# Row sums in three parts between additions, and a last copy shared by two engines

## The chip, the cores and the metric

The kernel runs on one core of a Trainium2 chip. A core has five engines with queues of their own: TensorE (matrix products, which end in PSUM), VectorE and ScalarE (element work; both read PSUM), GpSimd and SyncE (here they mostly issue transfers). Each engine works through its own queue in order and waits at an instruction until the counters named in it have been reached. The metric is the device time of one execution in microseconds.

## The reference

Two stages are joined. The first is a convolution along the sequence with weights that differ at each position: 8 batches of 4160 positions, 192 features in 8 heads, 7 taps. The weights of a position and head are a softmax over the 7 taps. The second stage takes each of the 33280 rows through two products to 1024 features, keeps the larger of the two, and multiplies by a third matrix.

```python
w = exp(weight_gen - max(weight_gen, axis=-1))
w = w / (sum(w, axis=-1) + 1e-09)                    # over the 7 taps
out = einsum('bshk,bskhg->bshg', w, windows(x_pad))  # 7 shifted copies of x
x = out.reshape(B * S, D)                            # 33280 x 192
out = maximum(x @ w1, x @ w2) @ w_out
```

## The kernel before

Each of the 128 partitions holds 260 consecutive rows, called columns. They are worked on in 17 batches: fifteen of 16 columns (0 to 14), one of 12 (15) and one of 8 (16). Work on a batch passes through all the engines.

- Weights: ScalarE takes the exponential of the batch (`exp_sum`, line 153). VectorE adds each run of 7 into `sum_t` (`red`, line 168, 8 sums per column). ScalarE takes the logarithm of the sums (`ln`, line 172). VectorE subtracts it from the raw weights (`shift`, line 177), and ScalarE takes the exponential again, which gives the normalised weights in bf16 (`weights`, line 191).
- Taps: VectorE multiplies the shifted copies of x by the weights (`mul`, line 211) and adds the 7 products in three additions (`adds`, lines 227, 233 and 236): 3 pairs, 2 pairs, and the last one, which writes `y_t`. The function `adds` takes a callback `beside(i, of)` and calls it ahead of each of the three additions, with i = 0, 1, 2 and of = 3. What the callback issues stands there in VectorE's queue.
- Transpose: a transposing transfer on SyncE's queue brings `y_t` into `yt`, features on the partitions. A small copy on GpSimd (`gate`, line 253) waits for it, and then GpSimd issues the next loads.
- Products: TensorE works through 260 tiles, three to a group (`hidden`). A tile is one chunk of 128 of the 1024 hidden features for the 8 columns of a unit (two chunks where a unit has 4 columns). With w2 - w1 in `wd`, max(h1, h2) is h1 + relu(x (w2 - w1)), so the kernel computes hidden tiles into the PSUM tiles hda, hdb and hdc (line 336), ScalarE takes their ReLU into `rd_t` (line 346), and the output is x (w1 w_out) plus the ReLU times w_out, summed in the PSUM tile op_ps (lines 388 and 376). ScalarE copies op_ps to `o_t` (`evac`, line 434), and SyncE stores it.

The order within a group g on TensorE is: hidden tiles a and b, the first output matmuls (`out_first`), hidden tile c, the second output matmuls (`out_second`). On ScalarE it is: ReLU a, ReLU b, a relay that waits for the first output matmuls and lets the second ones go, the softmax steps marked "before", ReLU c, the copy out of op_ps, the softmax steps marked "after". op_ps has a single buffer of two PSUM banks, as each of hda, hdb and hdc has, so the first output matmuls of a group wait until the copy of the group before has read it.

The softmax steps of ScalarE are placed by a table written out by hand, `SOFTMAX_AT`, with keys (group, 0 for before or 1 for after). The entry (16, 1), for example, holds l.5, the logarithm of batch 5. VectorE's order is written in `extra(t)`, called for each tile: the multiplications and additions of the next batch, with the subtractions of a later batch beside one half's additions and the sums of batch b + 3 beside the other half's. The first tiles of the program (16 of them) follow a list of their own, `OPENING`, of steps such as `lw.0.1` for a weight load.

A callback's part i of n is cut by `part` (line 157): columns n*i//of to n*(i+1)//of of the batch.

The results leave at the end by `rest_of_results`, and the very last pair of columns by a branch of `evac` of its own (lines 420 to 429): one copy on ScalarE of 2 x 192 columns out of two PSUM banks into `o_last`, and two stores, one on ScalarE's queue and one on SyncE's.

Of the kernel before, what the change touches and what calls it, by code (L numbers as in the profile page):

```python
# [9 lines left out]
FP32 = mybir.dt.float32  # L10
# [7 lines left out]
def _sub(base: bass.AP, off: int, dims):  # L18
    ap = [list(base.ap[0])] + [[int(s), int(c)] for s, c in dims]
    return dataclasses.replace(base, offset=base.offset + off, ap=ap)  # L20
# [3 lines left out]
def kernel(  # L24
# [9 lines left out]
    nc = tc.nc  # L34

    B, S, D = x.shape
    H, K = weight_gen.shape[2], weight_gen.shape[3]
    F = moe_w1.shape[1]
    P = 128
# [3 lines left out]
    HF = F // 2  # L43
# [8 lines left out]
    NB = len(BATCHES)  # L52

    def dcol(c):

        return (c + ROT) % CPP


    def pieces(b):
        n = BATCHES[b][1]  # L60
        at, done = [], 0
        for w in (4, 4, 4, 4) if b < 2 else (8, 8) if n == 16 else (8, 4) if n == 12 else (4, 4):
            at.append((done, w))
            done += w
        return at
# [14 lines left out]
    consts = ctx.enter_context(tc.tile_pool(name="consts", bufs=1))  # L80
# [76 lines left out]
    def part(b, i, of):  # L157

        n = BATCHES[b][1]
        c0, c1 = (4 * i, n if i else 4) if of == FIRST else (n * i // of, n * (i + 1) // of)  # L160
        h0, h1 = c0 * H, c1 * H
        return slice(h0, h1), h0 * K, [[K, h1 - h0], [1, K]]

    def red(b, i=0, of=1):
        if i == 0:
            s_ts[b] = psm.tile([P, BATCHES[b][1] * H], FP32, name="sum_t", tag="sum")
        hs, at, ap = part(b, i, of)
        nc.vector.reduce_sum(out=s_ts[b][:, hs], in_=_sub(e_ts[b], at, ap), axis=AX.X)  # L168
# [5 lines left out]
    def shift(b, i=0, of=1):  # L174
        hs, at, ap = part(b, i, of)
        w_t = _sub(wg_ts[b], at, ap)
        nc.vector.tensor_tensor(out=w_t, in0=w_t, in1=_sub(s_ts[b], hs.start, [[1, hs.stop - hs.start], [0, K]]),  # L177
                                op=ALU.subtract)
# [38 lines left out]
    def adds(b, o, first=False, beside=lambda i, of: None):  # L217


        w = dict(pieces(b))[o]  # L220
        n = w * D

        def taps(at, step, cnt):
            return _sub(m_t, K * o * D + at * n, [[step * n, cnt], [1, w * D]])

        beside(0, 3)
        nc.vector.tensor_tensor(out=taps(0, 1, 3), in0=taps(0, 1, 3), in1=taps(3, 1, 3), op=ALU.add)  # L227
        if first:
            return
        beside(1, 3)  # L230
        if b not in y_ts:
            y_ts[b] = py.tile([P, 16 * D], BF16, name="y_t", tag="y")
        nc.vector.tensor_tensor(out=taps(0, 2, 2), in0=taps(0, 2, 2), in1=taps(1, 5, 2), op=ALU.add)  # L233
        beside(2, 3)

        nc.vector.tensor_tensor(  # L236
            out=_sub(y_ts[b], o * D, [[64, 2], [P, 3 * w // 2], [1, 64]]),
            in0=taps(0, 1, 1), in1=taps(2, 1, 1), op=ALU.add,
        )
# [24 lines left out]
    def half(j):  # L264
        return slice(64 * j, 64 * j + 64)


    LEFT = (0, 1, 2, K - 1)

    def sum_transpose(u, i=None):  # L270

        b, o, n = UNITS[u]
        assert n == 4
        to = "h" if i == 0 else "o"
        yps = yps_of[u, i] = ps[to].tile([P, 1024], FP32, name="yps", tag="hd" if i == 0 else "op")
        ks = range(6) if i is None else range(3 * i, 3 * i + 3)
        for k in ks:
            for t in range(K):
                at = K * o * D + (t * 6 + k if i is None else (K * i + t) * 3 + k % 3) * P
                for r in range(2):  # L280
                    nc.tensor.matmul(  # L281
                        yps[:, r * 512 + k * 64:r * 512 + (k + 1) * 64],
                        lhsT=m_t[half(r), at:at + P], rhs=ident[half(r), half(r)],
                        start=(k == ks[0] and t == 0), stop=(t == K - 1),
                        skip_group_check=True,
                    )
# [62 lines left out]
    def column(c):  # L349

        for u, (b, o, n) in enumerate(UNITS):
            k = c - BATCHES[b][0] - o
            if 0 <= k < n:
                return u, k // 2, k % 2

    def place(p):

        u, i, _ = column(2 * p)
        b, o, n = UNITS[u]
        return BATCHES[b][0] + o + i, n // 2  # L360
# [55 lines left out]
    def evac(p, n):  # L416

        tile_, at = op_at[p]
        o = o_t[0]
        if p == NT // 2 - 1:  # L420

            nc.scalar.copy(out=_sub(o_last, 0, [[D, 2], [1, D]]),
                           in_=_sub(tile_, at, [[512, 2], [1, D]]))
            for j, eng in enumerate((nc.scalar, nc.sync)):
                eng.dma_start(
                    out=bass.AP(tensor=out.tensor, offset=dcol(place(p)[0] + 2 * j) * D, ap=[[CPP * D, P], [1, D]]),
                    in_=o_last[:, j * D:(j + 1) * D],
                )
            return
        runs = [[q for q in range(p, p + n) if column(2 * q)[0] == u]  # L430
                for u in range(column(2 * p)[0], column(2 * (p + n - 1))[0] + 1)]
        for qs in runs:
            c, h = place(qs[0])
            copied = nc.scalar.copy(out=_sub(o, c % 24 * D, [[D, len(qs)], [h * D, 2], [1, D]]),  # L434
                           in_=_sub(tile_, at + (qs[0] - p) * D, [[D, len(qs)], [512, 2], [1, D]]))
        stores = []
        for q in range(p, p + n):
            u, i, _ = column(2 * q)
            if u == NU - 2 and UNITS[u][2] == 8 and i % 2:
                stores.append((nc.sync, place(q)[0] - 1, [4 * D, 2], [1, 2 * D]))  # L440
            elif u < NU - 1 and i == UNITS[u][2] // 2 - 1:
                w = i + 1
                for k in range(0, 2 * w, w if u in PARTED else 2 * w):
                    stores.append((nc.sync, place(q)[0] - i + k, [1, (w if u in PARTED else 2 * w) * D]))
            if u == NU - 1:
                stores.append((nc.sync, place(q)[0], [2 * D, 2], [1, D]))
        for eng, c, *ap in stores:

            def issue(eng=eng, c=c, ap=ap, o=o):
                eng.dma_start(  # L450
                    out=bass.AP(tensor=out.tensor, offset=dcol(c) * D, ap=[[CPP * D, P], *ap]),
                    in_=_sub(o, c % 24 * D, ap),
                )

            if 3 <= u < NU - 3:
                held.append(issue)
            else:
                while u > 3 and held:
                    held.pop(0)()
                issue()  # L460
        return copied
# [81 lines left out]
    ident, swap = around[:, 0:P], around[:, 64:64 + P]  # L543
    zeros = consts.tile([P, PAD * D], BF16, name="zeros")
    gate = consts.tile([P, 1], FP32, name="gate")
    o_last = consts.tile([P, 2 * D], FP32, name="o_last")

    pstage = ctx.enter_context(ExitStack())
    stage = pstage.enter_context(tc.tile_pool(name="pstage", bufs=1))
# [2 lines left out]
    ws = {(kind, wi): stage.tile([P, w], FP32, name=f"ws{wi}{kind}") for kind, w in (("E", F), ("T", HF)) for wi in range(2)}  # L552
# [10 lines left out]
    def load_w(h, wi):  # L563

        wsrc = (moe_w1, moe_w2)[wi]
        return nc.sync.dma_start(
            out=ws["E", wi][:, h * HF:(h + 1) * HF],
            in_=bass.AP(tensor=wsrc.tensor, offset=h * HF, ap=[[F, P], [1, HF]]),
        )

    def load_last(h, wi):

        wsrc = (moe_w1, moe_w2)[wi]
        return nc.sync.dma_start(  # L574
            out=ws["T", wi][half(h), :],
            in_=bass.AP(tensor=wsrc.tensor, offset=P * F + h * HF, ap=[[F, 64], [1, HF]]),
        )
# [184 lines left out]
    def extra(t):  # L762

        u, k = TILES[t]
        b, o, n = UNITS[u]
        s = o + k

        if s == 0 and b + 1 < NB:
            mul(b + 1, 0)
        later = 0 if b < 4 else 5  # L770
        if s == later and b + 1 < NB:

            c = b + 1
            adds(c, 0, beside=lambda i, of: shift(c + 1, i, of) if c + 1 < NB else None)
        if s == 8 and b + 2 < NB:
            mul(b + 1, 8)
        if s == 8 + later and b + 2 < NB:
            adds(b + 1, 8, beside=lambda i, of: red(b + 3, i, 2) if b + 3 < NB and i < 2 else None)
        if s == 8 and b + 2 == NB:
            mul(b + 1, 4)  # L780
            adds(b + 1, 4)
        if k == n // 4 - 1 and 7 < u + 1 < NU:
            transpose(u + 1)

    def steps(g, tiles):

        for t in tiles:
            extra(t)
# [36 lines left out]
```

## Time and profile before

| | us |
|---|---|
| median of 3 runs | 405.34 (405.34 to 405.47) |
| the profiled execution's own time | 405.37 |
| its span | 403.6 |
| busy: TensorE | 394.8 (98%) |
| busy: VectorE | 369.1 (91%) |
| busy: ScalarE | 360.9 (89%) |

The profile is of one execution. The span runs from its first to its last recorded event; the time is a little longer. A row of a timeline gives start, length, engine, line, operation, tiles and shapes, and in brackets the idle time of the engine just before it with what ended it. A row of a group gives the count, then busy time, mean length in ns and idle time before. PE is TensorE, DVE VectorE, ACT ScalarE, POOL GpSimd; a q behind the name is an engine's queue of transfers. Lengths of VectorE and ScalarE rows overlap a little with the row behind, so costs are read from start to start; the ends of TensorE's rows are modelled.

### The profile page before, as it was taken

To read this page: it belongs to the slowest core of one execution; us is meant where nothing else is said; L and a number is where in the kernel's file an instruction comes from. 1 tells how busy PE (TensorE), PEld (TensorE's weight loads), DVE (VectorE), ACT (ScalarE), POOL (GpSimd) and SP (SyncE) were. 2 spreads that over 40 slices of the span, in tenths; PEclk is the share of its full clock that TensorE was granted. 3 is DMA by queue.
4 is the path that set the end of the run, shared out by engine and by line. 5 is a ranking of instruction groups with operands and counts; after the bars stand their busy time and mean duration, and the time that the engine had idled before them with its cause. 6 is when DMAs were issued, how large, how long until landed. Compare 5 with 4: busy or idle time off the path is not lost.

```text
span 403.6 us, 16321 instructions
## 1 busy us (share of the span) xinstructions
PE 394.8 (98%) x7499; PEld 321.3 (80%) x7499; DVE 369.1 (91%) x211; ACT 360.9 (89%) x466; POOL 72.3 (18%) x96
## 2 busy tenths in 40 slices
PE   7799999999999999999999999999999999999996
PEld 3589999777778777778777778877777877787996
DVE  5999999999999999999999999999999999998200
ACT  5999899999999989999899999989999899888872
POOL 3111031211122210222220122122012121200000
PEclk9999999999999999999999999999999999999999
DMA  8956468767768646864766667777457847558304
GB/s 262 222 140 151 120 124 167 183 164 133 190 110 222 182 79 129 240 187 80 217 187 107 141 192 193 99 215 198 81 115 228 178 80 200 141 106 193 104 31 169
DMA packets 60883, 63.16 MB, mean 157 GB/s; under 512 B 47641, under 2 KB 48665, under 8 KB 60816
## 3 DMA queue, kind: packets, MB, share of 16 engines
q1 hardware_dynamic: 52816, 40.15, 36.4%
q0 software_dynamic: 7856, 21.89, 27.4%
q8 instruction: 58, 0.95, 1.0%
q10 hardware_dynamic: 144, 0.10, 0.1%
q14 instruction: 9, 0.07, 0.1%
HBM read 36.55 MB, written 25.56 MB: 154 GB/s over the span
## 4 chain that ended last, share of the span: by engine, by line
PE 92%; ACT 5%; DMA 1%; SPq 1%; issue 0%
PE op_ps L376 42%; PE hdc L336 13%; PE hdb L336 13%; PE hda L336 13%; PE op_ps L388 8%; ACT rd_t L346 2%; DMA ws0E<-in_moe_w_dram 1%; PE hdp L336 1%; PE yps L281 1%; ACT en_t L191 1%; ACT yt L293 1%; ACT e_t L153 0%; ACT w1t L644 0%; SPq L574 0%; ACT w L622 0%
## 5 line engine op out<-in xcount | busy, mean ns | idle before, releaser
L376 PE MATMUL op_ps<-wo,rd_t 64*128 64x192 bf16 x4160 | 210.6, 243 | 0.0
L376 PEld LDWEIGHTS <-rd_t 64*128 64x128 bf16 x4160 | 181.0, 94 | 14.7
L211 DVE TENSOR_TENSOR m_t<-xb,en_t 128x10752 bf16<-128x10752 bf16 (+2 forms) x39 | 187.8, 4821 | 1.5 <-ACT en_t L191 1.4
L336 PEld LDWEIGHTS <-wd 64*128 64x128 bf16 x1824 | 96.8, 94 | 40.4 <-issue 2.5
L346 ACT ACTIVATE rd_t<-hdc 128x1024 bf16<-128x1024 f32 x82 | 84.1, 1025 | 17.8 <-PE hdc L336 16.2
L253 POOL CAST gate<-yt 128x1 f32<-128x1 bf16 x30 | 39.9, 1332 | 271.3 <-DMA yt<-y_t 271.3
L346 ACT ACTIVATE rd_t<-hda 128x1024 bf16<-128x1024 f32 x81 | 83.4, 1030 | 0.2 <-ACT o_t L434 0.2
L346 ACT ACTIVATE rd_t<-hdb 128x1024 bf16<-128x1024 f32 x81 | 83.5, 1031 | 0.0
L227 DVE TENSOR_TENSOR m_t<-m_t 128x4608 bf16<-128x4608 bf16 (+1 forms) x30 | 73.0, 2433 | 0.1
L336 PE MATMUL hdc<-yt,wd 64*128 64x512 bf16 (+1 forms) x552 | 67.9, 353 | 0.0
L434 ACT COPY o_t<-op_ps 128x384 f32<-128x384 f32 (+1 forms) x99 | 56.1, 577 | 12.4 <-PE op_ps L376 12.3
L336 PE MATMUL hdb<-yt,wd 64*128 64x512 bf16 (+1 forms) x540 | 67.1, 355 | 0.0
L336 PE MATMUL hda<-yt,wd 64*128 64x512 bf16 (+1 forms) x540 | 67.1, 355 | 0.0
L388 PE MATMUL op_ps<-w,yt 64*128 64x192 bf16 x780 | 55.5, 243 | 0.0
L388 PEld LDWEIGHTS <-yt 64*128 64x128 bf16 x780 | 39.0, 94 | 14.5 <-issue 0.3
L233 DVE TENSOR_TENSOR m_t<-m_t 128x3072 bf16<-128x3072 bf16 (+1 forms) x30 | 50.2, 1674 | 0.1
L191 ACT ACTIVATE en_t<-wg_t 128x896 bf16<-128x896 f32 (+3 forms) x48 | 35.7, 773 | 3.0 <-PE op_ps L376 2.0
L236 DVE TENSOR_TENSOR y_t<-m_t 128x1536 bf16<-128x1536 bf16 (+1 forms) x30 | 27.5, 916 | 0.6
L177 DVE TENSOR_TENSOR wg_t<-wg_t,sum_t 128x280 f32<-128x280 f32 (+6 forms) x46 | 22.2, 483 | 0.0
L168 DVE TENSOR_REDUCE sum_t<-e_t 128x64 f32<-128x448 f32 (+3 forms) x31 | 19.7, 639 | 2.3 <-ACT e_t L153 2.3
L125 POOL DMA_DIRECT2D xb<-in_x_dram x34 | 18.2, 537 | 17.3 <-ACT rd_t L346 11.0
L153 ACT ACTIVATE e_t<-wg_t 128x896 f32<-128x896 f32 (+2 forms) x18 | 15.9, 886 | 2.1 <-DMA wg_t<-in_weight_gen_dram 2.1
(40 smaller groups left out, 110.0 us busy)
## 6 DMA issues: line engine op xcount, KB each, us to landing
out_dram<-o_t SPq DMA_DIRECT2D x21, 768.0 KB, 4.3
xb<-in_x_dram POOLq DMA_DIRECT2D x30, 384.0 KB, 5.0
out_dram<-o_t SPq DMA_DIRECT2D x22, 384.0 KB, 3.7
wg_t<-in_weight_gen_dram POOLq DMA_DIRECT2D x13, 448.0 KB, 5.7
xb<-xb POOLq DMA_DIRECT2D x7, 288.0 KB, 5.1
wg_t<-in_weight_gen_dram SPq DMA_DIRECT2D x2, 448.0 KB, 5.2
xb<-in_x_dram POOLq DMA_DIRECT2D x4, 192.0 KB, 6.4
xs<-in_x_dram SPq DMA_DIRECT2D x1, 576.0 KB, 4.3
```

What stands on the lines that cost most here:

```text
L177: nc.vector.tensor_tensor(out=w_t, in0=w_t, in1=_sub(s_ts[b], hs.start, [[1, hs.stop - hs.start], [0, K]]), op=ALU.subtract)
L191: act = nc.scalar.activation(out=_sub(en_ts[b], (o * WGC + ((i or 0) * J + j) * N * K) * 2, [[2 * N, K], [2, N], [1, 2]]), in_=_sub(wg_ts[ ...
L211: return nc.vector.tensor_tensor(out=m_out, in0=x_in, in1=_sub(en_ts[b], at * H * 2, [[2, K * n * H], [0, G // 2], [1, 2]]), op=ALU.mult,)
L227: nc.vector.tensor_tensor(out=taps(0, 1, 3), in0=taps(0, 1, 3), in1=taps(3, 1, 3), op=ALU.add)
L233: nc.vector.tensor_tensor(out=taps(0, 2, 2), in0=taps(0, 2, 2), in1=taps(1, 5, 2), op=ALU.add)
L236: nc.vector.tensor_tensor(out=_sub(y_ts[b], o * D, [[64, 2], [P, 3 * w // 2], [1, 64]]), in0=taps(0, 1, 1), in1=taps(2, 1, 1), op=ALU.add,)
L253: nc.gpsimd.tensor_copy(out=gate, in_=yt[:, 0:1])
L336: nc.tensor.matmul(hid_out(t, f, j), lhsT=wd_at(j, s, f // 4, f % 4 * P, P), rhs=_sub(yt_ts[u][half(j), :], (s + j) % 3 * P, [[3 * P, w // ...
L346: relu_of[t0] = nc.scalar.activation(out=rd[:, k * 1024:(k + n) * 1024], in_=hd[:, at:at + n * 1024], func=AF.Relu)
L376: return nc.tensor.matmul(op_out(c), lhsT=rd[rows, k * 1024 + at:k * 1024 + at + P], rhs=wo[rows, f * D:(f + 1) * D], start=False, stop=(r ...
L388: nc.tensor.matmul(op_out(c + j), lhsT=yt_ts[u][half(j), (3 * i + (s + j) % 3) * P:(3 * i + (s + j) % 3 + 1) * P], rhs=w10[half(j), s * D: ...
L434: copied = nc.scalar.copy(out=_sub(o, c % 24 * D, [[D, len(qs)], [h * D, 2], [1, D]]), in_=_sub(tile_, at + (qs[0] - p) * D, [[D, len(qs)] ...
```

## The change

Sums: beside the additions of a batch's second half, `red` is now called in three parts, one ahead of each addition. Before it was called in two parts, ahead of the first and of the second addition. For 16 columns the parts were 8 and 8 columns (448 and 448 elements in) and are now 5, 5 and 6 (280, 280, 336).

Last copy: `o_last` becomes two tiles of 192 columns. ScalarE copies the first half and VectorE the second; ScalarE's queue stores the first, SyncE's the second.

Two more edits stand in the diff. `sum_transpose` sums four taps in place of seven where `adds` was called in its short form (`first`), for which a set `fewer` is kept; `load_w` and `load_last` learn a form for a whole row block and another queue. `OPENING` is not changed.

```diff
@@ adds
         if first:
+            fewer.add((b, o))
             return
@@
-    LEFT = (0, 1, 2, K - 1)
+    fewer = set()
@@ sum_transpose
+        taps = (0, 1, 2, K - 1) if (b, o) in fewer else range(K)
         for k in ks:
-            for t in range(K):
+            for t in taps:
@@ evac
-            nc.scalar.copy(out=_sub(o_last, 0, [[D, 2], [1, D]]),
-                           in_=_sub(tile_, at, [[512, 2], [1, D]]))
-            for j, eng in enumerate((nc.scalar, nc.sync)):
+            for j, (eng, copy) in enumerate(((nc.scalar, nc.scalar.copy), (nc.sync, nc.vector.tensor_copy))):
+                copy(out=o_last[j], in_=tile_[:, at + 512 * j:at + 512 * j + D])
                 eng.dma_start(
                     out=bass.AP(tensor=out.tensor, offset=dcol(place(p)[0] + 2 * j) * D, ap=[[CPP * D, P], [1, D]]),
-                    in_=o_last[:, j * D:(j + 1) * D],
+                    in_=o_last[j],
                 )
@@
-    o_last = consts.tile([P, 2 * D], FP32, name="o_last")
+    o_last = [consts.tile([P, D], FP32, name=f"o_last{j}") for j in range(2)]
@@ load_w
+        at, w = (0, F) if h == 2 else (h * HF, HF)
         return nc.sync.dma_start(
-            out=ws["E", wi][:, h * HF:(h + 1) * HF],
-            in_=bass.AP(tensor=wsrc.tensor, offset=h * HF, ap=[[F, P], [1, HF]]),
+            out=ws["E", wi][:, at:at + w],
+            in_=bass.AP(tensor=wsrc.tensor, offset=at, ap=[[F, P], [1, w]]),
         )
-    def load_last(h, wi):
+    def load_last(h, wi, act=0):
@@
-        return nc.sync.dma_start(
+        return (nc.scalar if act else nc.sync).dma_start(
@@ extra
         if s == 8 + later and b + 2 < NB:
-            adds(b + 1, 8, beside=lambda i, of: red(b + 3, i, 2) if b + 3 < NB and i < 2 else None)
+            adds(b + 1, 8, beside=lambda i, of: red(b + 3, i, 3) if b + 3 < NB else None)
```

## The prediction

> **What bounds the kernel now.** I read the page's busy shares first, then its groups, then the waits of TensorE and ScalarE after the opening, and last the timelines of the places that the change touches.
>
> ```profile
> span 403.6 us, 16321 instructions
> PE 394.8 (98%) x7499; PEld 321.3 (80%) x7499; DVE 369.1 (91%) x211; ACT 360.9 (89%) x466; POOL 72.3 (18%) x96
> L376 PE MATMUL op_ps<-wo,rd_t 64*128 64x192 bf16 x4160 | 210.6, 243 | 0.0
> ```
>
> TensorE is busy 98% of the span, and its largest group has no idle time ahead of it. From 60 us on, the list of what TensorE waited for is empty. So the end is set by TensorE's work plus the last copy and store. VectorE and ScalarE cost nothing unless one makes TensorE wait. VectorE is the engine to suspect: from about 39 us it runs without a gap to the end of its long work. The rows below say how far ahead of TensorE it still is late in the span.
>
> ```profile
> 349.83 1.75 POOL L253 CAST gate<-yt 128x1 f32<-128x1 bf16 x1 [9.17 <-DMA yt<-y_t]
> 351.83 0.83 PE L336 MATMUL hda<-yt,wd 64*128 64x512 bf16 x6
> ```
>
> GpSimd's gate starts when the transposed tile of batch 14's second half has landed; TensorE's first matmuls on that tile start 2.0 us later. VectorE's products arrive in time even there, by 2 us, so a faster VectorE shortens nothing, and up to 2 us more on it would be covered.
>
> **What the edits come to.** The set `fewer` stays empty, because no step of the opening asks for the short form of the additions; the new forms of the weight loads are not called either. These edits issue the same instructions as before, so they cost nothing and remove nothing. What is left is the sums and the last copy.
>
> **The sums on VectorE.** For batches 4 to 16 (13 of them) two reductions become three: 13 more instructions. In a batch of 16 columns, two of 448 elements become 280, 280 and 336. The rows below are one batch half with sums as it is now, and then the neighbouring half with three subtractions in the same places.
>
> ```profile
> 80.20 0.61 DVE L168 TENSOR_REDUCE sum_t<-e_t 128x64 f32<-128x448 f32 x1
> 80.73 2.55 DVE L227 TENSOR_TENSOR m_t<-m_t 128x4608 bf16<-128x4608 bf16 x1
> 83.20 0.62 DVE L168 TENSOR_REDUCE sum_t<-e_t 128x64 f32<-128x448 f32 x1
> 83.72 1.75 DVE L233 TENSOR_TENSOR m_t<-m_t 128x3072 bf16<-128x3072 bf16 x1
> 85.51 0.96 DVE L236 TENSOR_TENSOR y_t<-m_t 128x1536 bf16<-128x1536 bf16 x1
> ...
> 92.06 0.44 DVE L177 TENSOR_TENSOR wg_t<-wg_t,sum_t 128x280 f32<-128x280 f32 x1
> 92.42 2.56 DVE L227 TENSOR_TENSOR m_t<-m_t 128x4608 bf16<-128x4608 bf16 x1
> ...
> 95.24 1.75 DVE L233 TENSOR_TENSOR m_t<-m_t 128x3072 bf16<-128x3072 bf16 x1
> 96.91 0.50 DVE L177 TENSOR_TENSOR wg_t<-wg_t,sum_t 128x336 f32<-128x336 f32 x1
> 97.33 0.95 DVE L236 TENSOR_TENSOR y_t<-m_t 128x1536 bf16<-128x1536 bf16 x1
> ```
>
> From start to start the present half takes 0.53 + 2.47 + 0.52 + 1.79 = 5.31 us up to its third addition. The half with three subtractions takes 0.36 + 2.46 + 0.36 + 1.67 + 0.42 = 5.27. The third addition needs the second one's result: directly behind it, it starts 1.79 us after it; with a subtraction between, that subtraction starts after 1.67. A reduction of 336 lasts 0.50 us (the row at 316.87, below), the same as the subtraction of 336, so I price the new half as the subtracting half: 0.04 us less per batch, 0.5 us less on VectorE over 13 batches. Bounds: 1.6 us less over all, if only the 0.12 us of the waiting addition counts; 1.8 us more, if it isn't saved and each third reduction pays the part of a reduction that doesn't shrink with its size (0.61 for 448 and 0.50 for 336 leave about 0.14). All of it lies beside TensorE's work, under the 2.0 us above: nothing on the path.
>
> [...]
>
> **The logarithm that waits.** The sums feed one logarithm per batch on ScalarE (L172), placed by hand. Until now the last sum stood ahead of the second addition, now behind it. For batch 5 the third reduction starts at 80.20 - 0.04 (saved on batch 4) + 0.36 + 2.47 + 0.36 + 1.67 = 85.02 and ends at 85.52; today's second one ends at 83.20 + 0.62 = 83.82.
>
> ```profile
> 84.64 0.31 ACT L172 ACTIVATE sum_t<-sum_t 128x128 f32<-128x128 f32 x1
> 84.85 1.02 ACT L346 ACTIVATE rd_t<-hda 128x1024 bf16<-128x1024 f32 x1
> 85.75 1.03 ACT L346 ACTIVATE rd_t<-hdb 128x1024 bf16<-128x1024 f32 x1
> 86.75 1.02 ACT L346 ACTIVATE rd_t<-hdc 128x1024 bf16<-128x1024 f32 x1
> 87.67 0.47 ACT L434 COPY o_t<-op_ps 128x384 f32<-128x384 f32 x1
> ...
> 88.48 0.43 PE L388 MATMUL op_ps<-w,yt 64*128 64x192 bf16 x6
> ```
>
> ```profile
> 4.72 1.15 DVE L168 TENSOR_REDUCE sum_t<-e_t 128x64 f32<-128x448 f32 x2 [2.28 <-ACT e_t L153]
> 5.38 0.26 ACT L172 ACTIVATE sum_t<-sum_t 128x64 f32<-128x64 f32 x1 [0.22 <-DVE sum_t L168]
> ```
>
> ```profile
> 79.34 0.51 ACT L434 COPY o_t<-op_ps 128x384 f32<-128x384 f32 x1
> ...
> 79.90 0.42 PE L388 MATMUL op_ps<-w,yt 64*128 64x192 bf16 x6
> ```
>
> In the opening a logarithm starts about 0.05 us behind its reduction (4.72 + 0.61, then 5.38). So this one starts at 85.57 instead of 84.64: ScalarE stands still for 0.93 us. Queued behind it are the three ReLUs of the next group and the copy out of op_ps. At their present spacing (0.21, 0.90, then 0.91 and 0.92 without a wait) they start at 85.78, 86.68, 87.59 and 88.51; the copy ends at 88.98 where it ended at 88.14. The first output matmul of the group after that needs op_ps back. That it can start 0.05 us after such a copy is shown at 79.34 + 0.51 = 79.85 and 79.90. So it starts at 89.03 instead of 88.48: TensorE loses 0.55 us. The relay ahead of the second output matmuls (queued behind the ReLU at 86.68) may stop TensorE sooner, but that pause is part of the same 0.55, since the copy's end doesn't move with it. Lower bound: 0, if ScalarE's queue catches up; upper bound: the whole 0.93. I take 0.55, for op_ps has a single buffer and the rows have no other slack. TensorE has no later idle time to give it back.
>
> The other logarithms:
>
> ```profile
> 198.53 0.61 DVE L168 TENSOR_REDUCE sum_t<-e_t 128x64 f32<-128x448 f32 x1
> 203.25 0.31 ACT L172 ACTIVATE sum_t<-sum_t 128x128 f32<-128x128 f32 x1
> ```
>
> ```profile
> 245.87 0.61 DVE L168 TENSOR_REDUCE sum_t<-e_t 128x64 f32<-128x448 f32 x1
> 252.35 0.34 ACT L172 ACTIVATE sum_t<-sum_t 128x128 f32<-128x128 f32 x1
> ```
>
> ```profile
> 316.87 0.50 DVE L168 TENSOR_REDUCE sum_t<-e_t 128x48 f32<-128x336 f32 x1
> 320.90 0.28 ACT L172 ACTIVATE sum_t<-sum_t 128x96 f32<-128x96 f32 x1 [0.55 <-PE op_ps L376]
> 321.46 1.03 ACT L346 ACTIVATE rd_t<-hdc 128x1024 bf16<-128x1024 f32 x1 [0.28 <-PE hdc L336]
> ```
>
> Batch 10: the first reduction at 198.53 - 0.24, the last end 5.36 us later, 203.65. The logarithm would wait 0.45 us at its old time; but ScalarE and TensorE come 0.55 later, VectorE does not, so at 203.80 it finds its sums. Batch 12 (251.0 against 252.35) has more than 1 us, and so have the rest. Batch 15 (three reductions of 224 elements, about 5.1 us) ends near 321.55 against 320.90 + 0.55: up to 0.15 us, which the 0.28 us wait of the next ReLU covers. Nothing more is added.
>
> **The last copy.** The built program gives VectorE's copy one wait, on ScalarE's counter at the value that ScalarE's own half sets: both read the same op_ps tile. The halves follow each other; they do not run at once.
>
> ```profile
> 399.95 0.39 SPq L450 DMA_DIRECT2D out_dram<-o_t  x1
> 400.05 0.48 ACT L422 COPY o_last<-op_ps 128x384 f32<-128x384 f32 x1
> 400.56 0.34 SPq L425 DMA_DIRECT2D out_dram<-o_last  x1
> 400.56 0.37 ACTq L425 DMA_DIRECT2D out_dram<-o_last  x1
> ```
>
> ```profile
> 400.90:401.50 0.60, 0.00 (x0) 1.00 0.97 319
> 401.50:402.10 0.60, 0.00 (x0) 1.00 0.94 314
> ```
>
> ```profile
> L667 ACT CAST w<-pw 64x192 bf16<-64x192 f32 x2 | 0.6, 314 | 0.0
> L177 DVE TENSOR_TENSOR wg_t<-wg_t,sum_t 128x224 f32<-128x224 f32 x3 | 1.2, 385 | 0.0
> ```
>
> ScalarE's 192 columns take 0.31 us instead of 0.48, so its store is issued at 400.40, 0.16 earlier. VectorE has no copy out of PSUM in this trace; between 0.31 (ScalarE, same size) and 0.39 (a subtraction of 224) I take 0.35: from 400.41 to 400.76, and SyncE's store at 400.79, 0.23 later than now. What does that do to the end? The stage table (length, ScalarE's busy time, clock, DMA share, GB/s) shows the 16 DMA engines full from 400.9 to 402.1 with the store issued at 399.95 and these two. Issue to full flow is about 0.9 us (399.95 to 400.9), so SyncE's 96 KB flow from about 401.7, and at 319 GB/s need 0.3 us: 402.0, inside the present 402.1. I take 0; bounds 0.16 less and 0.23 more. Nothing is queued behind the two waiting stores but the end of the program.
>
> **Sum.** 0.55 + 0 + 0: the span goes from 403.6 to 404.15 us. The profiled execution took 405.37, 1.8 more than its span and 0.03 above the median of 405.34. On the median that is 405.9 us, 0.14% slower. A change below 0.2% (0.8 us) is about what a measurement of this kernel can't tell from none.
>
> **The rivals.**
> - The whole stall reaches TensorE. Its place is op_ps behind the logarithm of batch 5, its price 0.93 us, and with the late store of SyncE 1.16: 406.3 to 406.5, slower. It decides once the 0.34 us between the copy's end (88.14) and the matmul (88.48) hide less than 0.1. For it: the single buffer. Against: the pair at 79.85 and 79.90, which shows that 0.05 is enough.
> - The stall is absorbed: ScalarE runs early or the reductions end sooner; then 405.2 to 405.4. Against: ReLU rows at 84.85 to 87.67 without gaps.
> - The stall as forecast, and SyncE's store is late by its 0.23: 406.1. For it: the series. Against: full DMA engines.
> - The halves run at once: 0.55 - 0.16 gives 405.7. The Trainium skill, PSUM — Partial Sum Buffer (PSUM bank collisions raise a hardware error), has reads of different banks by two engines run clean; the halves lie in two banks. The wait in the program stands against it, and no row here shows it.
> - VectorE's tiles do hold TensorE: 0.5 us less, and no stall seen: 404.8. Against: the 2.0 us.
>
> **Chances.** Forecast 0.52, full stall 0.14, absorbed 0.14, late store 0.13, halves at once 0.03, VectorE the bound 0.04. The first, third, fourth and fifth lie within 0.2%, less a few hundredths at the edge of 406.15: same 0.78, slower 0.17, faster 0.05. The range 405.2 to 406.5 reaches from the absorbed to the full stall.
>
> **What would show it.** In the changed profile: a logarithm of batch 5 near 85.6 with a wait on L168 of 0.8 to 0.9 us; the output matmuls after it near 89.0; from there every TensorE row 0.5 to 0.6 later; 44 reductions; third additions 0.42 behind a reduction; VectorE's last copy behind ScalarE's. I am wrong if TensorE's rows past 90 us keep their times, if several logarithms wait, or if the last store ends more than 0.2 us later after the last matmul.

## The result and the profile after

The changed kernel takes 408.58 us (median of 8 executions, 407.28 to 410.62) against 405.4 us before: ratio 1.0078, 95% interval 1.0053 to 1.0102. It is slower by 0.8%; the forecast was 405.9 us, at most 406.5. The profiled execution took 409.53 us with a span of 407.8, so it holds 4.2 us more of span than the profiled execution of before.

These are the span, the busy shares and two groups on the page of the changed kernel:

```profile
span 407.8 us, 16334 instructions
PE 396.8 (97%) x7499; PEld 320.5 (79%) x7499; DVE 369.3 (91%) x225; ACT 360.2 (88%) x466; POOL 184.2 (45%) x96
...
L254 POOL CAST gate<-yt 128x1 f32<-128x1 bf16 x30 | 151.8, 5060 | 163.7 <-DMA yt<-y_t 163.7
...
L211 DVE TENSOR_TENSOR m_t<-xb,en_t 128x10752 bf16<-128x10752 bf16 (+2 forms) x39 | 187.8, 4821 | 12.2 <-ACT rd_t L348 9.2
```

The same gate group stood on the page of before like this:

```profile
L253 POOL CAST gate<-yt 128x1 f32<-128x1 bf16 x30 | 39.9, 1332 | 271.3 <-DMA yt<-y_t 271.3
```

VectorE and ScalarE are as busy as before (369.3 against 369.1 us, 360.2 against 360.9). The number that moved is GpSimd's: 184.2 us instead of 72.3, all of it in the gate, a copy of one column whose mean length went from 1.33 to 5.06 us. And VectorE's multiplications (L211) have 12.2 us of idle time ahead of them.

The waits of the changed kernel from 60 us to the end show what follows from that (engine, line, what it waited for; total us, times, longest us):

```profile
DVE m_t L211 <- ACT rd_t L348: 9.2, 1, 9.2
...
ACT sum_t L172 <- DVE sum_t L168: 4.7, 3, 2.2
DVE m_t L211 <- DMA xb<-xb: 2.8, 2, 1.7
...
PE op_ps L390 <- ACT o_t L435: 1.3, 3, 0.5
```

Three logarithms wait for their sums (4.7 us), where the forecast had one; VectorE waits for loads of x, which nobody had forecast. (The 9.2 us stands at 375.76, near the end of VectorE's work. The list puts it down to ScalarE's ReLU, but nearly all of it belongs to a long gate; the rows are further down.)

Matching TensorE's 7499 rows of both traces one by one shows where the changed kernel falls behind, as steps in the difference of starts:

| place (time in the trace of before) | TensorE later by | what it waits for |
|---|---|---|
| opening, up to 17 us | 1.2 us | loads of the weights |
| 88.5 | 0.49 | logarithm of batch 5 |
| 205 to 207 | 1.4 | logarithm of batch 10 |
| 323.9 | 0.7 | logarithm of batch 15 |
| 380 to 386 | 0.43 | the transposed tile yt |

The sum is 4.2 us. The first line belongs to this execution and not to the change: the opening's code issues the same instructions, and in the other profiles below the opening stands between 0.2 us early and 0.5 us late. Without it 3.0 us are left, which agrees with the medians (408.58 - 405.4 = 3.2).

Batch 5 in the changed kernel, as the forecast had it (all 1.2 us later than there because of the opening):

```profile
86.19 0.50 DVE L168 TENSOR_REDUCE sum_t<-e_t 128x48 f32<-128x336 f32 x1
86.60 0.95 DVE L237 TENSOR_TENSOR y_t<-m_t 128x1536 bf16<-128x1536 bf16 x1
86.72 0.31 ACT L172 ACTIVATE sum_t<-sum_t 128x128 f32<-128x128 f32 x1 [0.77 <-DVE sum_t L168]
...
89.65 0.49 ACT L435 COPY o_t<-op_ps 128x384 f32<-128x384 f32 x1
90.19 0.42 PE L390 MATMUL op_ps<-w,yt 64*128 64x192 bf16 x6 [0.31 <-ACT o_t L435]
```

And batch 10, which was to find its sums (a later window of the same timeline):

```profile
136.71 5.76 DVE L211 TENSOR_TENSOR m_t<-xb,en_t 128x10752 bf16<-128x10752 bf16 x1 [1.72 <-DMA xb<-xb]
...
206.24 0.50 DVE L168 TENSOR_REDUCE sum_t<-e_t 128x48 f32<-128x336 f32 x1
206.78 0.31 ACT L172 ACTIVATE sum_t<-sum_t 128x128 f32<-128x128 f32 x1 [1.72 <-DVE sum_t L168]
...
210.24 0.42 PE L390 MATMUL op_ps<-w,yt 64*128 64x192 bf16 x6 [0.46 <-ACT o_t L435]
```

VectorE has lost time at 136.71, where a multiplication starts 1.72 us late because its x is not there; by batch 10 its sums come too late and TensorE pays. Why x is late is seen where a load is issued. The clearest place is an earlier one. These rows are VectorE's and GpSimd's in the changed kernel from the third addition of batch 4's second half on:

```profile
62.59 0.50 DVE L168 TENSOR_REDUCE sum_t<-e_t 128x48 f32<-128x336 f32 x1
63.00 0.95 DVE L237 TENSOR_TENSOR y_t<-m_t 128x1536 bf16<-128x1536 bf16 x1
63.86 5.75 DVE L211 TENSOR_TENSOR m_t<-xb,en_t 128x10752 bf16<-128x10752 bf16 x1
69.28 12.19 POOL L254 CAST gate<-yt 128x1 f32<-128x1 bf16 x1 [9.85 <-DMA yt<-y_t]
69.53 0.45 DVE L177 TENSOR_TENSOR wg_t<-wg_t,sum_t 128x280 f32<-128x280 f32 x1
...
75.68 5.75 DVE L211 TENSOR_TENSOR m_t<-xb,en_t 128x10752 bf16<-128x10752 bf16 x1
81.35 0.44 DVE L168 TENSOR_REDUCE sum_t<-e_t 128x40 f32<-128x280 f32 x1
81.42 0.53 POOL L125 DMA_DIRECT2D xb<-in_x_dram  x1
```

And here is the same place in the kernel before:

```profile
60.06 1.75 DVE L233 TENSOR_TENSOR m_t<-m_t 128x3072 bf16<-128x3072 bf16 x1
61.85 0.96 DVE L236 TENSOR_TENSOR y_t<-m_t 128x1536 bf16<-128x1536 bf16 x1
62.72 5.75 DVE L211 TENSOR_TENSOR m_t<-xb,en_t 128x10752 bf16<-128x10752 bf16 x1
68.02 0.49 POOL L253 CAST gate<-yt 128x1 f32<-128x1 bf16 x1 [9.81 <-DMA yt<-y_t]
68.39 0.44 DVE L177 TENSOR_TENSOR wg_t<-wg_t,sum_t 128x280 f32<-128x280 f32 x1
68.56 0.53 POOL L125 DMA_DIRECT2D xb<-in_x_dram  x1
```

In both kernels the gate's transfer lands late in a long multiplication (5.75 us). Before, the copy ends 0.12 us after the next VectorE instruction has started (68.02 + 0.49 = 68.51 against 68.39). After the change, it does not get in there. It passes six further instructions of VectorE and a second long multiplication, and ends 0.12 us after a reduction has started (69.28 + 12.19 = 81.47 against 81.35). The load of x queued behind it on GpSimd (L125) is issued at 81.42 instead of 68.56. This first late load costs VectorE only 0.15 us at its next multiplication (87.69). The wait of 1.72 us at 136.71 comes about in the same way: a gate starts at 115.54 and lasts 13.37 us, and the loads behind it are issued from 128.85 on.

The 9.2 us near the end are such a wait too:

```profile
353.41 10.25 POOL L254 CAST gate<-yt 128x1 f32<-128x1 bf16 x1 [6.50 <-DMA yt<-y_t]
```

Behind this gate GpSimd issues loads at 363.60 and 364.12, and when the second has landed, at 371.23, the last transfer into x (L145), which lands 4.4 us later, at about 375.6; the multiplication starts at 375.76. In the run below that has the new sums and the old copy, the gate at this place got in early (352.35, 2.67 us), and the same multiplication waited 0.80 us. So over 8 of the 9.2 us belong to the gate. TensorE's last step (380 to 386) is what reaches TensorE of this wait.

The Trainium skill, SBUF — State Buffer (SBUF: two separate sides), states that VectorE and GpSimd have one port pair in common, that a VectorE instruction with two operands in SBUF competes for it with a GpSimd instruction that reads SBUF, that whichever starts first holds it for the whole instruction, and that the other is fully blocked. Multiplications, additions and subtractions here have two such operands, a reduction has one; that the copy gets through at a reduction, 0.12 us after its start, agrees. What the Trainium skill does not say there, and the trace shows, is that the hold can outlast the instruction: here eight VectorE instructions, one directly behind the other, keep the copy out, for 12 us. So the question of the experiments was which part of the change does this, and through what.

### The profile page after: what moved, and what is told of

Read it like the earlier page. It is cut to its first block, busy times and chain, and to the rows that moved or that the text cites. A ratio compares the mean times of both kernels' runs of the same rounds, so it can differ in the third digit from the quotient of the medians.

```text
span 407.8 us, 16334 instructions
## 1 busy us (share of the span) xinstructions
PE 396.8 (97%) x7499; PEld 320.5 (79%) x7499; DVE 369.3 (91%) x225; ACT 360.2 (88%) x466; POOL 184.2 (45%) x96
## 4 chain that ended last, share of the span: by engine, by line
DVE 61%; DMA 11%; PE 11%; issue 10%; ACT 5%; SPq 0%; POOL 0%; DVEq 0%; POOLq 0%; ACTq 0%
DVE m_t L211 28%; DVE m_t L227 14%; DVE m_t L234 10%; PE op_ps L378 5%; DVE y_t L237 5%; DMA yt<-y_t 4%; DMA xb<-xb 3%; ACT rd_t L348 3%; DVE wg_t L177 2%; DVE sum_t L168 2%; DMA wg_t<-in_weight_gen_dram 2%; DMA ws0T<-in_moe_w_dram 2%; PE hdc L338 1%; PE op_ps L390 1%; DMA xb<-zeros 1%
## 5 line engine op out<-in xcount | busy, mean ns | idle before, releaser
L254 POOL CAST gate<-yt 128x1 f32<-128x1 bf16 x30 | 151.8, 5060 | 163.7 <-DMA yt<-y_t 163.7
L211 DVE TENSOR_TENSOR m_t<-xb,en_t 128x10752 bf16<-128x10752 bf16 (+2 forms) x39 | 187.8, 4821 | 12.2 <-ACT rd_t L348 9.2
L125 POOL DMA_DIRECT2D xb<-in_x_dram x34 | 18.2, 537 | 18.8 <-ACT rd_t L348 10.9
L168 DVE TENSOR_REDUCE sum_t<-e_t 128x40 f32<-128x280 f32 (+6 forms) x44 | 21.7, 494 | 2.2 <-ACT e_t L153 2.2
```

The lines of the kernel that those rows point to most:

```text
L211: return nc.vector.tensor_tensor(out=m_out, in0=x_in, in1=_sub(en_ts[b], at * H * 2, [[2, K * n * H], [0, G // 2], [1, 2]]), op=ALU.mult,)
L254: nc.gpsimd.tensor_copy(out=gate, in_=yt[:, 0:1])
```

## The experiments

The theory was formed in this order: first which of the two edits loses the time, then whether the gate is the carrier, then what in VectorE's queue shuts the gate out. Each median stands beside that of executions of the kernel before, taken together with it on the same chip.

**One edit at a time.** The first run has the changed kernel's last copy and the old sums, the second the reverse.

```diff
e1: adds(b + 1, 8, beside=lambda i, of: red(b + 3, i, 2) if b + 3 < NB and i < 2 else None)
e2: adds(b + 1, 8, beside=lambda i, of: red(b + 3, i, 3) if b + 3 < NB else None)
e2: o_last = consts.tile([P, 2 * D], FP32)      # one copy on ScalarE, as before
...
```

> Sums in two parts as before, last copy shared as in the change. Both theories, starved gate and late logarithms, put nothing here: 405.2 to 405.7, the last row of SyncE's store about 0.4 us later behind the last matmul than before, no gate on GpSimd longer than 2 us. If the copy were part of the loss, 406 or more.

> Sums in three parts, last copy as before. Both theories: the whole loss, 407 to 410, with gates of 10 to 14 us in the trace and three logarithms that wait for VectorE. If the copy had a part in it, less than that.

The copy alone: 405.46 against 405.48 us, ratio 1.0006 (0.9995 to 1.0017). The sums alone: 408.82 against 405.48, ratio 1.0093 (1.0070 to 1.0116). The sums carry the whole loss, the copy none, though it runs as a series just as forecast. The end of the changed kernel:

```profile
404.29 0.32 ACT L425 COPY o_last<-op_ps 128x192 f32<-128x192 f32 x1
404.64 0.36 DVE L425 COPY o_last<-op_ps 128x192 f32<-128x192 f32 x1 [17.09 <-ACT o_last L425]
405.02 0.34 SPq L426 DMA_DIRECT2D out_dram<-o_last  x1
```

VectorE's half starts when ScalarE's has ended, and SyncE's store is issued 0.73 us behind the first half's start, 0.22 us later than before (400.05 to 400.56), where about 0.4 was expected. In the run with the copy alone TensorE's rows past 20 us stand within 0.1 us of before, and the span is 403.4 us against 403.6: the end does not move.

**The gate taken away.** If the late loads carry the loss, the change without a copy as gate must lose only the forecast's stall. Here an empty instruction of GpSimd waits for the transposing transfer in place of the copy.

```diff
-        nc.sync.dma_start_transpose(
+        turned_yt = nc.sync.dma_start_transpose(
...
-        nc.gpsimd.tensor_copy(out=gate, in_=yt[:, 0:1])
+        go = nc.gpsimd.nop()
+        tc.add_manual_dep(go.ins, turned_yt.ins.name, SYNC, reason="loads behind the transpose")
```

> The whole change, but GpSimd's gate is a bare wait for the transposed tile and reads no SBUF. Theory starved gate: the loads are issued when the tile lands, VectorE never waits for x, the logarithms of batches 10 and 15 find their sums, and only the 0.5 us of batch 5 is left: 405.6 to 406.2. Rival, the late logarithms alone cost it and the long gate rows are harmless: 407.5 to 410 as before.

It took 406.1 us against 405.48, ratio 1.0016 (1.0007 to 1.0025). Past 60 us TensorE falls behind before's trace at one place only, by 0.49 us at 88.5. The timeline at batch 5 in this run:

```profile
85.98 0.31 ACT L172 ACTIVATE sum_t<-sum_t 128x128 f32<-128x128 f32 x1 [0.76 <-DVE sum_t L168]
...
89.45 0.42 PE L391 MATMUL op_ps<-w,yt 64*128 64x192 bf16 x6 [0.31 <-ACT o_t L436]
```

So with the gate out of the way the forecast's step is all that is left.

**Is it the reading of SBUF?** The gate as a GpSimd instruction that only writes SBUF:

```diff
...
-        nc.gpsimd.tensor_copy(out=gate, in_=yt[:, 0:1])
+        go = nc.gpsimd.memset(gate, 0.0)
+        tc.add_manual_dep(go.ins, turned_yt.ins.name, SYNC, reason="loads behind the transpose")
```

> The whole change, with GpSimd's gate as a fill of its one column (it writes SBUF and reads none) that waits for the same transposed tile. If it is the gate's read of SBUF that VectorE shuts out: fills below 0.3 us each and 405.7 to 406.3. If any use of SBUF by GpSimd is shut out: fills of 10 to 14 us and 407 to 410.

It took 406.0 us against 405.68, ratio 1.0004 (0.9987 to 1.0020). Every gate lasts 0.10 us, beside the same VectorE instructions:

```profile
67.95 0.10 POOL L254 MEMSET gate<- 128x1 f32 x1 [10.88 <-DMA yt<-y_t]
```

A write gets in at once where a read is kept out for 12 us. That is the distinction which the Trainium skill draws in SBUF — State Buffer (SBUF: two separate sides), and this run agrees.

**What in the sums shuts it out?** Three parts differ from two in that a reduction now stands between the second and the third addition. Two runs put a reduction there in the kernel before whose result nothing reads, one of 7 elements and one of 140:

```diff
+    tiny = consts.tile([P, 1], FP32)        # e5: spare, [P, 20]
+    def tiny_red(b):                        # e5: _sub(e_ts[b], 0, [[K, 20], [1, K]])
+        nc.vector.reduce_sum(out=tiny, in_=e_ts[b][:, 0:K], axis=AX.X)
-            adds(b + 1, 8, beside=lambda i, of: red(b + 3, i, 2) if b + 3 < NB and i < 2 else None)
+            adds(b + 1, 8, beside=lambda i, of: (red(b + 3, i, 2) if i < 2 else tiny_red(b + 3)) if b + 3 < NB else None)
```

> The kernel before with one more reduction of 7 elements (to a scratch value nobody reads) between the second and the third addition: sums and logarithms stay where they were, only VectorE's pause ahead of the third addition is filled. Theory starved gate, which hangs on that pause: gates of 10 to 14 us, loads late, 406 to 409. Rival, late logarithms: 405.2 to 405.6 and gates below 2 us.

> The kernel before with a spare reduction of 140 elements (20 sums that nobody reads) between the second and the third addition. It is about 0.2 us long, longer than the 0.12 us by which the third addition had to wait, so the addition now starts directly behind it, about 0.865 us ahead of the next multiplication instead of 0.875. Sums and logarithms stay where they were; VectorE has some 1.2 us more to do in all, under its 2.0 us of lead. Theory that the direct start shuts the gate out: gates of 10 to 14 us in the halves with subtractions, loads late, VectorE waiting for x, 406 to 409. Rival, the gates follow the place or the size of the sums: gates below 3 us and 405.2 to 405.8.

The tiny reduction did nothing: 405.52 against 405.48, ratio 1.0002 (0.9991 to 1.0012), every gate under 3 us. My expectation of long gates was wrong. The larger one cost the time: 408.28 against 405.68, ratio 1.0064 (1.0041 to 1.0087), with gates up to 13.6 us. First the run with the tiny reduction, at the place shown above:

```profile
61.90 0.15 DVE L765 TENSOR_REDUCE tiny<-e_t 128x1 f32<-128x7 f32 x1
62.02 0.96 DVE L236 TENSOR_TENSOR y_t<-m_t 128x1536 bf16<-128x1536 bf16 x1
62.89 5.75 DVE L211 TENSOR_TENSOR m_t<-xb,en_t 128x10752 bf16<-128x10752 bf16 x1
68.30 0.38 POOL L253 CAST gate<-yt 128x1 f32<-128x1 bf16 x1 [9.91 <-DMA yt<-y_t]
```

Then the run with the spare reduction of 140:

```profile
59.85 1.75 DVE L233 TENSOR_TENSOR m_t<-m_t 128x3072 bf16<-128x3072 bf16 x1
61.52 0.29 DVE L765 TENSOR_REDUCE spare<-e_t 128x20 f32<-128x140 f32 x1
61.73 0.94 DVE L236 TENSOR_TENSOR y_t<-m_t 128x1536 bf16<-128x1536 bf16 x1
62.59 5.75 DVE L211 TENSOR_TENSOR m_t<-xb,en_t 128x10752 bf16<-128x10752 bf16 x1
67.82 12.38 POOL L253 CAST gate<-yt 128x1 f32<-128x1 bf16 x1 [9.81 <-DMA yt<-y_t]
```

The third addition needs the second one's result. Directly behind it (before), it starts 1.79 us after it, where an instruction that needs nothing starts after 1.67 (59.85 to 61.52): VectorE pauses for 0.12 us. The tiny reduction takes 0.12 us from start to start (61.90 to 62.02) and fits into the pause; the spare one takes 0.21 and fills it. The unrounded starts in the trace show a difference at the next instruction as well: the multiplication L211 starts 0.875 us behind an addition that came out of the pause and 0.865 us behind one that did not. From here the theory was that this pause decides, although it lies 6 us ahead of the gate.

In the run with the spare reduction the loss reaches TensorE by another way than in the changed kernel. Its sums keep their places, and no logarithm holds TensorE up. Of the 3.3 us that TensorE falls behind there after the opening, 2.6 come at 381 to 386, where it waits for the transposed tile yt: one gate (352.52, 10.13 us) has left VectorE without x for 8.9 us. So late loads are what the two kernels have in common; whether the logarithms or the product tiles hand them on to TensorE differs.

**The pause against other differences.** Two more runs on the kernel before. One puts the tiny reduction behind the third addition, so that the multiplication directly follows a reduction but the addition keeps its pause. The other puts a spare addition of two 140-element operands where the spare reduction stood, so that the pause is filled with no reduction. Neither result is read.

```diff
e9:  after adds(b + 1, 8, ...):  if b + 3 < NB: tiny_red(b + 3)
e10: between the additions:      nc.vector.tensor_tensor(out=spare, in0=e[:, 0:140], in1=e[:, 140:280], op=ALU.add)
```

> The kernel before with a reduction of 7 elements (to a scratch value) behind the third addition instead of ahead of it, so the third addition keeps its pause of 0.12 us and the next multiplication starts directly behind a reduction. Theory that a pause of VectorE inside the last three instructions is what lets the gate in: gates below 3 us, 405.2 to 405.8. Rival, a two-input instruction directly behind a reduction shuts the gate out: gates of 10 to 14 us and 406 to 409.

> The kernel before with a spare addition of 140 fp32 elements (two inputs, a result that nobody reads) between the second and the third addition, where another run had a spare reduction. Theory that the missing pause shuts the gate out, whatever fills it: gates of 10 to 14 us, 406 to 409. Rival, only a reduction there does it: gates below 3 us and 405.2 to 405.8.

With the pause kept: 405.83 against 405.83, ratio 0.9995 (0.9985 to 1.0006), no gate of 2 us or more (the longest lasts 1.93). With the pause filled by an addition: 408.85 against 405.83, ratio 1.0068 (1.0050 to 1.0085), with eight gates of 12.3 to 13.6 us. It is the pause and not the kind of instruction that fills it. Rows of the run with the spare addition:

```profile
62.06 0.29 DVE L766 TENSOR_TENSOR spare<-e_t 128x140 f32<-128x140 f32 x1
...
68.37 12.38 POOL L253 CAST gate<-yt 128x1 f32<-128x1 bf16 x1 [9.81 <-DMA yt<-y_t]
```

**An opening for the gate where it is kept out.** In the whole change, a reduction of 7 elements ahead of the first subtraction, since a reduction was where the gate got in:

```diff
-  adds(c, 0, beside=lambda i, of: shift(c + 1, i, of) if c + 1 < NB else None)
+  adds(c, 0, beside=lambda i, of: (tiny_red(c + 1) if i == 0 else None, shift(c + 1, i, of)) if c + 1 < NB else None)
```

> The whole change, and ahead of the first subtraction of each half a reduction of 7 elements (to a scratch value nobody reads), directly behind the multiplication. Theory that the gate gets in where VectorE runs a reduction and is shut out between two-input instructions: every gate ends about 0.13 us behind the start of the instruction after a multiplication, none above 3 us, and 405.7 to 406.3, as with the bare wait. Rival, the gate is slow for another reason: long gates remain, 407 to 410.

It took 408.55 us against 405.68, ratio 1.0076 (1.0063 to 1.0089): no gain, and my expectation was missed. The gates did become short, except one that arrived just too late for the opening:

```profile
257.74 0.15 DVE L767 TENSOR_REDUCE tiny<-e_t 128x1 f32<-128x7 f32 x1
257.79 11.96 POOL L254 CAST gate<-yt 128x1 f32<-128x1 bf16 x1 [10.70 <-DMA yt<-y_t]
...
278.46 5.76 DVE L211 TENSOR_TENSOR m_t<-xb,en_t 128x10752 bf16<-128x10752 bf16 x1 [2.63 <-DMA xb<-xb]
...
324.81 0.28 ACT L172 ACTIVATE sum_t<-sum_t 128x96 f32<-128x96 f32 x1 [3.41 <-DVE sum_t L168]
...
326.80 0.42 PE L390 MATMUL op_ps<-w,yt 64*128 64x192 bf16 x6 [1.72 <-ACT o_t L435]
```

That one gate, 0.05 us behind the reduction's start, costs VectorE 2.63 us at its next x, the logarithm of batch 15 waits 3.41 us, and TensorE loses 1.9 us there. So a single late load is enough for most of the loss. That the executions of the changed kernel spread over 3 us would fit this, since which gates are kept out depends on when transfers land; no run separates it.

**The stall of 0.5 us.** The change with the empty instruction as gate, and the logarithms of batches 5 and 10 one place later in ScalarE's table:

```diff
-  (16, 1): "l.5"   ...  (44, 1): "l.10"
+  (17, 0): "l.5"   ...  (45, 0): "l.10"
```

> The whole change, with GpSimd's gate as a bare wait, and the logarithms of batches 5 and 10 one half group later in ScalarE's table. If the 0.5 us left with the bare wait are the logarithm of batch 5, no TensorE row past 60 us shifts against before by more than 0.2 us, and the time is that of before: 405.2 to 405.6. If something else costs them: 405.9 to 406.2.

It took 405.63 us against 405.68, ratio 0.9991 (0.9971 to 1.0011). The step at 88.5 us is gone, so it was the place of the logarithm. VectorE's saving buys nothing either: this is the time of before.

**The change with its pause given back.** The last run keeps the gate's copy and the three parts, and only moves the third part behind the third addition; three logarithms stand one place later.

```diff
-  adds(b + 1, 8, beside=lambda i, of: red(b + 3, i, 3) if b + 3 < NB else None)
+  adds(b + 1, 8, beside=lambda i, of: red(b + 3, i, 3) if b + 3 < NB and i < 2 else None)
+  if b + 3 < NB: red(b + 3, 2, 3)
   (16, 1): "l.5" -> (17, 0)     (44, 1): "l.10" -> (45, 0)     (72, 0): "l.15" -> (72, 1)
```

> The whole change with its sums in three parts, but the third part stands behind the third addition instead of ahead of it, so that this addition directly follows the second one and keeps its pause; GpSimd's gate is the copy that reads yt, as in the change. Since the last sum now ends about 1 us later, three logarithms stand one place later on ScalarE (batches 5, 10 and 15). Theory (the filled pause shuts the gate out): every gate lasts under 3 us, no load is late, 405.5 to 406.1 us against 405.8 of the kernel before, although VectorE issues as many reductions of the same size as the changed kernel. Rival (three reductions between VectorE's long instructions shut the gate out wherever the third stands): gates of 11 us or more, 407.5 to 409.

It took 405.67 us against 405.48, ratio 1.0008 (0.9989 to 1.0027). The same reductions stand in the same half; the addition has its pause (60.05 to 61.83 is 1.78) and no gate lasts longer than 2.3 us:

```profile
60.05 1.75 DVE L234 TENSOR_TENSOR m_t<-m_t 128x3072 bf16<-128x3072 bf16 x1
61.83 0.96 DVE L237 TENSOR_TENSOR y_t<-m_t 128x1536 bf16<-128x1536 bf16 x1
62.71 0.49 DVE L168 TENSOR_REDUCE sum_t<-e_t 128x48 f32<-128x336 f32 x1
63.12 5.75 DVE L211 TENSOR_TENSOR m_t<-xb,en_t 128x10752 bf16<-128x10752 bf16 x1
68.38 0.53 POOL L254 CAST gate<-yt 128x1 f32<-128x1 bf16 x1 [9.83 <-DMA yt<-y_t]
```

Four profiled executions keep the pause: before, e4 and e9 (the tiny reduction between the additions and behind them) and e11 (the third part behind). In them there are 52 long multiplications ahead of subtractions, in which a gate arrives: all 52 gates end at the first boundary, 0.12 to 0.13 us into the next instruction. Four fill it: the changed kernel, e2 (the sums alone), e5 and e10 (the spare reduction and the spare addition). In them there are 34 without another wait: all 34 gates are kept out. In 14 more of these four runs the multiplication itself started late, after a wait for x, and there the gate is let in again. When the gate arrives does not tell the two groups apart: 3.5 to 5.5 us into the multiplication where it gets in, 4.0 to 5.4 where it doesn't. Of the 34, 32 end 0.12 to 0.13 us into a reduction, as at 81.35. The other two (353.41 in the changed kernel, 352.52 in e5) meet no reduction; they end 0.01 us into an addition that needs the product just before it and starts 0.03 to 0.04 us after that has ended, so out of a pause.

## Why the prediction was wrong

- **The dead edits and the last copy cost nothing**: right. The copy alone measured 1.0006. VectorE's half took 0.36 us (taken: 0.35) and waited for ScalarE's; the late store of SyncE is hidden. The rivals of a late store and of halves that run at once fall.
- **VectorE's 13 more reductions take no more time**: right as a sum. A half takes 81.35 to 86.60 = 5.25 us up to its third addition, against 5.31 before (forecast: 5.27). One bound was worked out too low: 0.61 us for 448 elements and 0.50 for 336 leave 0.17 us that doesn't shrink, not 0.14, which would have put the upper bound at 2.2 us, over the 2.0 of cover. The half measured 5.25 us, far from that bound. The 0.5 us saved is worth nothing, as said; the run with the logarithms moved and no gate shows it at 0.9991.
- **The stall of batch 5**: the mechanism was right and the size near. The logarithm waited 0.76 to 0.77 us (forecast 0.93), the output matmul came 0.48 to 0.49 us later (forecast 0.55). Alone, it gives the 406.1 and 406.0 us of the runs with another gate; the forecast was 405.9. The rival of a stall that reaches TensorE whole falls, and so does the absorbed one.
- **"All of it lies beside TensorE's work, under the 2.0 us above: nothing on the path"**: this step failed. I priced the reductions by VectorE's own time alone, and saw the pause of 0.12 us only as time saved. I quoted the gate's row (1.75 us for a copy of one column) as a clock for yt's arrival and did not ask why so small a copy takes that long: it was waiting for VectorE. The pause was what let it end at the first boundary. Without it, gates last 10 to 13.6 us, the loads queued behind them on GpSimd come late, and VectorE waits for x. Nor do the 2.0 us cover what TensorE waits for: they are the lead of the product tiles, and in the changed kernel most of the loss goes through the sums, whose lead is smaller (next point). The failed step is worth 408.82 - 406.1 = 2.7 us, by the run with the sums alone and the one without the copy as gate.
- **Batches 10 and 15 find their sums**: wrong, as a consequence, and the forecast's own sign of being wrong (several logarithms wait) came up. By its sum batch 10 had 0.15 us in hand (203.65 against 203.80) if VectorE kept its times. VectorE was later by the waits for x (2.8 us in all), so batch 10 cost TensorE 1.4 us and batch 15 cost 0.7. With the gate replaced, neither waits long enough to move TensorE, as forecast.

Shown by the runs: the sums carry the loss, the gate's read carries it to the loads, and filling or keeping the pause switches it on or off. Not shown is what inside the chip makes a pause two instructions earlier decide whether a read of GpSimd gets in 6 us later; no run here tells more than the association, 52 against 34 without an exception.

## What to carry to other kernels

When a small GpSimd instruction lasts far longer than its work, ask what it is shut out by before packing VectorE's queue tighter: a filled pause can cost more than it saves, and the price is paid in the transfers queued behind GpSimd. A GpSimd instruction that only has to wait for a transfer should not read SBUF; an empty instruction or a memset with the dependency did the same without being shut out. And when sums move later, move what consumes them in the other engine's table too: one place was worth 0.5 us here.

## What was unexpected of the hardware

- A copy of one column on GpSimd was kept out for 12.19 us, over eight VectorE instructions that follow each other directly, and got in 0.12 us after a one-input reduction started; a memset at the same place took 0.10 us.
- Where a multiplication stands ahead of a subtraction and starts without a wait, the gate's fate went with whether VectorE had paused for 0.12 us ahead of the addition before that multiplication. The instruction behind that addition starts 0.875 to 0.878 us after it with the pause and 0.864 to 0.870 without it.
- An opening is short: a gate that arrived 0.05 us after a 7-element reduction had started missed it and lasted 11.96 us.
